# Moving the planned side work of an interleaved attention and Fourier kernel from the start of a section to behind its last tile

## The chip, the cores and the metric

The kernel runs on one core of a Trainium2 chip. The metric is the device time of one execution in microseconds (us); lower is better. Times of unprofiled runs are given as a median over several runs. A profiled execution is a run of its own, with its own time, and its trace gives start and length of every instruction.

A core has five engines, each with its own instruction stream that it works through in order. In the profile PE is TensorE (matmuls), PEld its weight loads, DVE is VectorE, ACT is ScalarE, POOL is GpSimd, and SP is SyncE, which only issues DMAs here. Engines wait for each other through semaphores.

## The reference

Two branches work on the same input `x` (2048 tokens of width 512, float32) and are mixed by a gate per token:

```python
g = _sigmoid((x * gate_w).sum(-1, keepdims=True))
# branch A: Fourier mixing, real part of DFT over tokens of DFT over width
a = einsum("bsd,ed->bse", x, hid_re); b = einsum("bsd,ed->bse", x, hid_im)
A = einsum("ts,bse->bte", seq_re, a) - einsum("ts,bse->bte", seq_im, b)
# branch B: attention with 32 heads of width 16
p = softmax(einsum("bhqd,bhkd->bhqk", q, k) * 16 ** -0.5)
B = einsum("bhqk,bhkd->bhqd", p, v).reshape(B, S, D) @ wo
out = g * A + (1 - g) * B
```

## The kernel before

Every operand that needs more precision than one pass gives is held as a high part and a rest (`hi_lo`: a copy on ACT, a subtraction on DVE or POOL), and a product is three matmuls. The first part of the kernel projects `x` to queries, keys and values and writes queries and keys to DRAM. From there on all stages are interleaved by hand: the schedule is manual, so each engine executes in the order in which the Python code issues.

**Attention.** Two heads make a pair, 16 pairs in all. Pair `p` has its queries and keys in the buffers `qs[p % 2]` and `ks[p % 2]`, 64 rows a head; `load_stacks(p)` (line 196) fills them with 12 DMAs of 128 KB from SP. Three kinds of tiles follow.

- An `a` tile (`a_tile`, line 211) is a product of queries and keys on PE whose row maximum DVE reduces (line 219). When half of a pair's rows are through, `m_parts` and `m_rows` are put into `deferred`; one of them is run at the end of a section. They form the negated maximum and write it as two extra rows into `qs`, by four small DMAs from SP (first head) and four from POOL (second head), line 240.
- An `s` tile (`scores`, line 669) is the product of keys and queries with these rows in it (line 682), and ACT takes the exponential out of PSUM (line 683).
- Value products (`pv`, line 708): for two key blocks ("units"), 8 products of exponentials and values into one PSUM bank (line 718). ACT copies the bank to `oe` (two buffers, line 727), or for the first pair of units of a half straight to `osum` (line 724). The addition of `oe` to `osum` on POOL is put into the list `adds` (line 728) and issued later by `add_sums` (line 738); the last of a half also issues two DMAs that write `osum` to DRAM (line 736).

A unit is one pair, one half of the query rows and one block of 128 keys: 512 units in all. `valued` counts the units whose value products are issued.

**Sections.** `segment` (line 850) runs one pattern of slots: single slots issue a matmul of the other branch (the "d" matmuls of line 378: Fourier products, later output projections) on one half of the PE's rows and, beside it, an `s` or `a` tile of one head on the other half. Each section has 8 `s` and 8 `a` tiles. The last slot, "|", issues what was held back of the Fourier branch (`late`), then `values()` with `pv` for two units. Below, "section N" is the section during which `valued` is N when it starts; it ends with the value products of units N and N+1. 26 sections with the pattern `THIN` (N = 2 to 52) run beside the width transform, 192 with `FULL` (54 to 436) beside the token transform, and 26 with `NINE` (438 to 488) beside projections. Of the eight PSUM banks in use one holds the "d" products; seven rotate over `s` and `a` tiles and value products, in an order that a small planner (`bank`, `read_by`, lines 343 to 359) picks while the code issues; its estimates depend on slots alone.

**Token transform.** Its weights come in chunks: `c_load` (line 319, DMA from SP into `craw`, two buffers) and `c_split` (line 325, high part and rest on POOL, three buffers). After the last matmul of a chunk, `dft_next` (line 426) issues `c_split` for three chunks later and `c_load` for five later, in the even-halved sections (N divisible by 4). Each third such section also ends a row block: ACT takes it out of PSUM (lines 432 and 435), and in the second half of the transform POOL adds the first half's result (line 436).

**Planned steps.** The normalisation of finished attention rows is put into a table `plan`, each entry with the unit at which it is due; `run_plan(u)` issues what is due up to `u + 1`. Before, `run_plan(valued)` stands ahead of every section (line 911).

```python
last = 32 * (4 * ct + n - 1) + 16 * (hf + 1)
at(last + (4 if ct < 3 else 2), sums, hf, ct, n)
at(last + (12 if ct < 3 else 4), inverse, hf, ct, n)
if ct < 3:
    for half in range(2):
        for step, du in enumerate((16, 20, 22)):
            at(last + du + 8 * half, block, step, hf, ct, half)
for p in range(1, NP):
    at(32 * (p - 1), load_stacks, p)
at(456, load_yg, 0, range(3)); at(481, load_yg, 0, range(3, 8))
for step, u in enumerate((486, 490, 494)):
    at(u, last_block, step, 1, 3, nc.gpsimd)
```

`sums` (line 473) gathers the sums of exponentials by two small DMAs into `rc`; `inverse` (line 481) takes the reciprocal on DVE and writes it back by two DMAs; `block` step 0 (line 507) loads a block of rows and its reciprocals by four DMAs into `no`, step 1 multiplies them on POOL (line 515), step 2 casts the product into `nh` on ACT, subtracts on POOL (lines 83 and 84 in `hi_lo`) and stores it by a DMA (line 520). With six combinations of `hf` and `ct` and two halves there are 12 blocks, so 12 casts on ACT, at the starts of sections 134, 142, 150, 158, 262, 270, 278, 286, 390, 398, 406 and 414. `last_block` and `load_yg` do the like for the last pairs and load the mixed Fourier rows.

After the sections comes a tail (line 915 on) for the last units, with its own calls of `add_sums` and `run_plan` ahead of each two units.

Of the kernel before, what the change touches and what calls it, by code (L numbers as in the profile page):

```python
# [31 lines left out]
def mix_kernel(ctx: ExitStack, tc: tile.TileContext, xa_t, xa, wqkv, w_hid, w_seq, wo, gate_w, out):  # L32
# [654 lines left out]
    def pv_last(u):  # L687
        nonlocal now
        blk, k2 = divmod(u - UNITS + 16, 8)
        pt = pts.pop(u)  # L690
        if k2 == 0:
            i, acc = bank()
            free[i] = 1e9
            held[:] = [i]
            last_pairs.append(LastPair(blk, acc))
        acc = last_pairs[-1].acc
        for j in range(4):
            x, h = divmod(j, 2)
            nc.tensor.matmul(acc[32 * j:32 * j + 32], vt[:, 2 * k2 + x, NP - 1, h:h + 32], pt[:, j],  # L699
                             start=k2 == 0, stop=k2 == 7)  # L700
        now += 3.75
        if blk == 0 and k2 == 7:
            last_pairs[0].copy(1)
            free[held[0]] = now + 6
# [3 lines left out]
    def pv(us):  # L708

        nonlocal now  # L710
        i, acc = bank()
        for u in us:
            p, r = divmod(u, 32)
            hf, kt = divmod(r, 16)
            pt = pts.pop(u)
            for j in range(4):
                h = j % 2
                nc.tensor.matmul(acc[32 * j:32 * j + 32], vt[:, kt, p, h:h + 32], pt[:, j],  # L718
                                 start=u == us[0], stop=u == us[-1])
        now += 3.75 * len(us) + 1  # L720
        read_by(i, "s")
        o = osum[:, hf]
        if kt + 1 == len(us):
            nc.scalar.copy(o, acc)
            return
        oe = work.tile([P, 512], F32, name="oe", bufs=2)
        nc.scalar.copy(oe, acc)  # L727
        adds.append(partial(add_sum, o, oe, p, hf, kt == NT - 1))
# [9 lines left out]
    def add_sums():  # L738
        while adds:
            adds.pop(0)()  # L740
# [14 lines left out]
    def issue(x, half, stop=True, late=None):  # L755
        nonlocal now
        now += half is None
        chain, st, mv, after, last = x
        i = chain.mm(st, mv, half, last and stop)
        if stop and after:  # L760
            if last and late is not None:
                late.append(after)
            else:
                after()
        return i

    def pump(gen, n):
        for x in take(gen, n, False):
            issue(x, None)
# [34 lines left out]
    def run_plan(u):  # L804
        for v in sorted(v for v in plan if v <= u + 1):
            for f in plan.pop(v):
                f()
# [19 lines left out]
    users, valued = [], 0  # L827

    def score(kind, h):
        x = next(streams[h][kind == "a"], None)  # L830
        if x:
            if kind == "a":
                i, ps = bank()
                read_by(i, "a")
                users.append((kind, a_tile(*x, ps)))
            else:
                users.append((kind, scores(*x)))

    def values():
        nonlocal valued  # L840
        us = valued, valued + 1
        valued += 2
        add_sums()
        if us[0] < UNITS - 16:
            pv(us)
        else:
            for u in us:
                pv_last(u)

    def segment(pattern, half, ds, stop):  # L850


        nonlocal now
        nonlocal users
        before, users = users, []
        ds, late = iter(ds), []
        for slot in pattern.split():
            if slot == "|":
                for f in late:
                    f()  # L860
                values()
                continue
            now += 1
            if len(slot) == 1:
                x = next(ds, None)
                if x:

                    before = before if x[0].begun else None
                    i = issue(x, half, stop, late)
                    users = []  # L870
                    if before:
                        tc.add_manual_dep(
                            i.ins, dict(before).get("s", before[0][1]).ins.name,
                            mybir.DependencyInfo(mybir.DependencyClass.Sync, mybir.DependencyReason.DATA))
                        before = None
            score(slot[0], 1 - half)
            if len(slot) == 2:
                score(slot[1].lower(), half)
        if deferred:
            deferred.pop(0)()  # L880

    def pairs():

        for i in range(NT - 3):
            yield (THIN,) * 2, take(hid, 12)
        for i in range(2 * NT * 3):
            yield (FULL,) * 2, take(seq, 16)
        for gen, n in ((proj(1, (0, 1, 2), one), 8), (first, 5)):
            for i in range(n):
                yield NINE, take(gen, 9)  # L890
# [5 lines left out]
    for i in range(6):  # L896
        pump(hid, 6)
        if i < 4:
            for kind in "sa":
                for h in range(2):  # L900
                    score(kind, h)
        else:
            if i == 4:
                values()
            for _ in range(2):
                score("s", 0)
                score("a", 0)
    users = []
    for patterns, ds in pairs():
        for half in range(2):  # L910
            run_plan(valued)
            segment(patterns[half], half, ds, half == 1)


# [9 lines left out]
    for u in range(valued + 2, UNITS, 2):  # L924
        add_sums()
        run_plan(u)
        for i in range(4):
            if i == 2:
                pump(*whole[u])
                if u == 506:  # L930
                    last_pairs[0].turn()
                elif u == 508:
                    last_pairs[0].back()
            for h in range(2):
                scores(u + i // 2, i % 2, h)
        if u == 510:
            last_pairs[0].products(())
        values()
# [38 lines left out]
```

## Time and profile before

| | us |
|---|---|
| time, median of 3 unprofiled runs | 1710.47 (1710.4 to 1710.5) |
| the profiled execution's own time | 1713.87 |
| its span, first to last instruction | 1712.1 |
| PE busy (matmuls) | 1693.7 |
| DVE busy | 1376.3 |
| ACT busy | 1247.9 |
| POOL busy | 715.4 |

The span is what the views of the trace divide up; the profiled execution's time has 1.8 us around it. Matmuls overlap, so the share of PE's busy time says that it seldom stands still for long, not that it runs at its peak: a stretch in which matmuls start later shows in the length of a section rather than in idle time. The useful unit of reading is therefore the section, measured from one start of value products (line 718) to the next.

### The profile page before, as it was taken

What the parts mean: (1) busy time and instruction counts of PE and PEld (TensorE: products, weight loads), DVE (VectorE), ACT (ScalarE), POOL (GpSimd) and SP (SyncE); (2) the same over time, 40 slices, a digit from 0 to 9 for tenths busy, and PEclk for the clock granted to TensorE, in tenths of its full rate; (3) what the DMA queues carried; (4) which work ended last, traced back from release to release, by engine and by line L of the source; (5) the groups of instructions that cost most, each with busy time, mean ns of one, the idle gap of its engine ahead of it and who ended that gap; (6) DMA issues with size and microseconds to landing.
All of it is one profiled execution on the core that took longest, in us unless ns stands there. A gap on an engine that the chain in (4) does not pass through costs nothing.

```text
span 1712.1 us, 33831 instructions
## 1 busy us (share of the span) xinstructions
PE 1693.7 (99%) x12731; PEld 1081.6 (63%) x12731; DVE 1376.3 (80%) x2298; ACT 1247.9 (73%) x2472; POOL 715.4 (42%) x775
## 2 busy tenths in 40 slices
PE   8999999999999999999999999999999999999997
PEld 7876666666666666666666666666666656555543
DVE  5448788888888888888888888888888888799943
ACT  5212288887787788778788788778778778778785
POOL 0211144454444455444444555545455555322230
PEclk9999999999999999999999999999999999999999
DMA  8972511314141525232146635241322535560114
GB/s 280 341 173 98 159 16 19 46 32 81 53 80 46 95 89 103 60 67 59 40 92 247 125 94 108 57 87 51 72 73 66 106 100 101 183 151 8 39 27 136
DMA packets 82484, 165.12 MB, mean 96 GB/s; under 512 B 19776, under 2 KB 20032, under 8 KB 78480
## 3 DMA queue, kind: packets, MB, share of 16 engines
q1 hardware_dynamic: 77968, 162.56, 37.1%
q8 instruction: 100, 1.64, 0.4%
q0 software_dynamic: 4352, 0.39, 0.3%
q14 instruction: 64, 0.52, 0.1%
HBM read 107.73 MB, written 54.52 MB: 95 GB/s over the span
## 4 chain that ended last, share of the span: by engine, by line
PE 97%; DVE 1%; DMA 1%; issue 0%; POOL 0%; ACT 0%; SPq 0%; DVEq 0%; POOLq 0%; ACTq 0%
PE d L378 38%; PE t L718 27%; PE t L217 11%; PE t L682 9%; PE t L87 4%; PE t L88 3%; PE t L89 3%; PE t L699 1%; DVE mx L219 1%; PE t L378 0%; DMA qs<-mt 0%; DMA raw<-wqkv 0%; DVE yp L559 0%; PE t L637 0%; DMA o<-osum 0%
## 5 line engine op out<-in xcount | busy, mean ns | idle before, releaser
L219 DVE TENSOR_REDUCE mx<-t 128x1 f32<-128x512 f32 x2048 | 1267.4, 682 | 218.2 <-PE t L217 185.0
L683 ACT ACTIVATE pt<-t 128x512 f32<-128x512 f32 x2048 | 1034.9, 632 | 14.4 <-PE t L682 10.5
L682 PE MATMUL t<-qs,ks 50*128 50x512 f32 x2048 | 745.0, 414 | 3.6 <-DMA qs<-mt 2.4
L217 PE MATMUL t<-ks,qs 48*128 48x512 f32 x2048 | 695.5, 404 | 0.3 <-DVE mx L219 0.2
L378 PE MATMUL d<-xab,ch 64*128 64x512 f32 x2016 | 648.6, 396 | 0.0
L718 PE MATMUL t<-pt,vt 128*32 128x512 f32 x3968 | 478.9, 600 | 0.0
L378 PEld LDWEIGHTS d<-xab,ch 64*128 64x128 f32 x2016 | 367.1, 185 | 131.7 <-issue 90.7
L217 PEld LDWEIGHTS t<-ks,qs 48*128 48x128 f32 x2048 | 366.4, 186 | 79.0 <-DVE mx L219 26.3
L378 PE MATMUL d<-xab,cl 64*128 64x512 f32 x1008 | 399.4, 396 | 0.0
L682 PEld LDWEIGHTS t<-qs,ks 50*128 50x128 f32 x2048 | 367.6, 185 | 39.4 <-ACT pt L683 12.6
L733 POOL TENSOR_TENSOR osum<-osum,oe 128x512 f32<-128x512 f32 x217 | 278.9, 1285 | 124.4 <-ACT oe L727 118.5
L727 ACT COPY oe<-t 128x512 f32<-128x512 f32 x217 | 127.3, 587 | 254.1 <-PE t L718 252.5
L718 PEld LDWEIGHTS t<-pt,vt 128*32 128x32 f32 x3968 | 105.1, 109 | 230.2 <-issue 149.9
L333 POOL CAST ch<-craw 128x512 fp32r<-128x512 f32 x126 | 77.0, 611 | 377.9 <-PE t L682 364.5
L378 PEld LDWEIGHTS d<-xab,cl 64*128 64x128 f32 x1008 | 186.2, 185 | 67.5 <-issue 53.6
L334 POOL TENSOR_TENSOR cl<-craw,ch 128x512 fp32r<-128x512 f32 x126 | 162.1, 1286 | 10.2
L240 POOL DMA_DIRECT2D qs<-mt x128 | 72.0, 568 | 101.5 <-DVE mt L236 94.6
L83 ACT CAST hl<-t 128x512 fp32r<-128x512 f32 x48 | 28.1, 586 | 85.2 <-PE t L89 67.3
L378 PE MATMUL d<-wre,xab 64*128 64x512 f32 (+1 forms) x348 | 85.5, 391 | 0.1
L378 PE MATMUL d<-wo_hl,o_hl 64*128 64x512 f32 (+1 forms) x261 | 69.7, 393 | 0.0
L378 PEld LDWEIGHTS d<-wre,xab 64*128 64x128 f32 (+1 forms) x348 | 64.0, 185 | 7.0 <-issue 1.1
L84 DVE TENSOR_TENSOR hl<-t,hl 128x512 fp32r<-128x512 f32 x48 | 32.9, 687 | 37.6 <-ACT hl L83 37.6
(115 smaller groups left out, 890.8 us busy)
## 6 DMA issues: line engine op xcount, KB each, us to landing
craw<-w_seq SPq DMA_DIRECT2D x128, 256.0 KB
qk<-hl SPq DMA_DIRECT2D x32, 512.0 KB
qs<-qk SPq DMA_DIRECT2D x96, 128.0 KB
ks<-qk SPq DMA_DIRECT2D x96, 128.0 KB
b<-hl SPq DMA_DIRECT2D x16, 512.0 KB
xab<-b SPq DMA_DIRECT2D x16, 512.0 KB
o<-osum SPq DMA_DIRECT2D x62, 128.0 KB
oh<-nh SPq DMA_DIRECT2D x12, 512.0 KB
```

Of the source, the lines that this page charges most:

```text
L87: nc.tensor.matmul(ps, sh, mh, start=first, stop=False)
L217: nc.tensor.matmul(ps, qs[p % 2][r, qt * P:(qt + 1) * P], ks[p % 2][r, kb * 512:(kb + 1) * 512], start=True, stop=True)
L219: user = nc.vector.tensor_reduce(mx[p % 2][:, h, qt, kb:kb + 1], ps, AX.X, ALU.max)
L240: (nc.sync, nc.gpsimd)[h].dma_start(rows.rearrange("v (q b c) -> v b q c", q=8, b=4)[:, b], mt[hf][32 * b + h:32 * b + 32:2])
L333: nc.gpsimd.tensor_copy(h1, raw)
L334: nc.gpsimd.tensor_tensor(l1, raw, h1.bitcast(F32), ALU.subtract)
L378: i = nc.tensor.matmul(self.ps, st[r], mv[r], start=not self.begun, stop=stop)
L682: nc.tensor.matmul(ps, ks[p % 2][rr, kt * P:(kt + 1) * P], qs[p % 2][rr, q0:q0 + 512], start=True, stop=True)
L683: return nc.scalar.activation(pts[u][:, 2 * qb + h], ps, AF.Exp, bias=0.0, scale=DH ** -0.5)
L718: nc.tensor.matmul(acc[32 * j:32 * j + 32], vt[:, kt, p, h:h + 32], pt[:, j], start=u == us[0], stop=u == us[-1])
L727: nc.scalar.copy(oe, acc)
L733: nc.gpsimd.tensor_tensor(o, o, oe, ALU.add)
```

## The change

The call of `run_plan(valued)` ahead of every section goes away. At the "|" slot of `segment`, behind the section's last tile and its held-back Fourier steps, the code now issues the additions of value sums, then the planned steps that are due, then the value products. `valued` has the same value at both places, so an entry that was issued ahead of section N's first tile is now issued behind section N's last tile and ahead of its value products. `add_sums` leaves `values()`; the one other caller of `values()` ahead of the sections gets its own call, and the tail loop has one already. The call of `run_plan` at the start of the tail stays.

```diff
     def values():
         nonlocal valued
         us = valued, valued + 1
         valued += 2
-        add_sums()
         if us[0] < UNITS - 16:
             pv(us)
         else:
@@
             if slot == "|":
                 for f in late:
                     f()
+                add_sums()
+                run_plan(valued)
                 values()
                 continue
@@
             if i == 4:
+                add_sums()
                 values()
@@
         for half in range(2):
-            run_plan(valued)
             segment(patterns[half], half, ds, half == 1)
```

On ACT the order in a section with a cast was: copy of the value sums of the section before, cast, 8 exponentials; it is now: 8 exponentials, cast, copy of this section's value sums. On DVE a planned reciprocal moves from ahead of the section's 8 reductions to behind them (and behind a held-back `finish` where there is one). On POOL planned products and differences now stand behind the section's `c_split` and addition. On SP planned DMAs now stand behind the section's `c_load` and, where a half of a pair is complete, behind the two DMAs that write `osum`. PE executes the same instructions in the same order.

## The prediction

> **What bounds the kernel now.** I read the page's engine totals and the shares of the chain that ended last, then the lengths of single sections.
>
> ```profile
> PE 1693.7 (99%) x12731; PEld 1081.6 (63%) x12731; DVE 1376.3 (80%) x2298; ACT 1247.9 (73%) x2472; POOL 715.4 (42%) x775
> PE 97%; DVE 1%; DMA 1%; issue 0%; POOL 0%; ACT 0%; SPq 0%; DVEq 0%; POOLq 0%; ACTq 0%
> ```
>
> PE holds 97% of the chain, and the change gives PE nothing and takes nothing from it: its instructions and their order stay. So time can only move where PE's matmuls start late because another engine has not freed a bank or delivered an operand. Matmuls overlap, so such a delay shows as a longer section, not as idle PE. I therefore took the windows view, each stretch from one start of value products to the next, for the 12 sections that begin with a cast (one of them and the sum of all 12), and next for the 12 sections just ahead of these (likewise).
>
> ```profile
> 1368.60:1374.93 6.33, 6.33 (x50) 3.30 (x49) 5.48 (x10) 5.03 (x11) 5.59 (x5) 1.00 0.23 81
> ...
> sum 75.86, PE 75.86 PEld 39.35 DVE 65.56 ACT 62.48 POOL 61.68; mean PE 6.32 PEld 3.28 DVE 5.46 ACT 5.21 POOL 5.14
> ```
> ```profile
> 1362.79:1368.60 5.81, 5.81 (x49) 3.81 (x48) 5.50 (x11) 4.49 (x10) 3.59 (x6) 1.00 0.03 3
> ...
> sum 69.84, PE 69.84 PEld 45.17 DVE 61.54 ACT 53.90 POOL 35.56; mean PE 5.82 PEld 3.76 DVE 5.13 ACT 4.49 POOL 2.96
> ```
>
> The first number after a stretch is its length. Sections with a cast take 6.32 us in the mean, their neighbours 5.82: 0.50 us each, 75.86 - 69.84 = 6.02 us in all. PE counts as busy throughout in both. Why it is the cast: ACT's and DVE's timelines in section 398, which lies between the value products that start at 1368.60 and 1374.93.
>
> ```profile
> 1370.65 0.59 ACT L727 COPY oe<-t 128x512 f32<-128x512 f32 x1 [1.30 <-PE t L718]
> 1371.13 0.62 ACT L83 CAST nh<-no 128x512 fp32r<-128x512 f32 x1
> 1371.65 4.02 ACT L683 ACTIVATE pt<-t 128x512 f32<-128x512 f32 x8
> 1376.97 0.59 ACT L727 COPY oe<-t 128x512 f32<-128x512 f32 x1 [1.30 <-PE t L718]
> ```
> ```profile
> 1371.24 4.99 DVE L219 TENSOR_REDUCE mx<-t 128x1 f32<-128x512 f32 x8 [0.82 <-PE t L217]
> 1377.56 0.69 DVE L219 TENSOR_REDUCE mx<-t 128x1 f32<-128x512 f32 x1 [1.33 <-PE t L217]
> ```
>
> A section is a ring on ACT: copy of the value sums, 8 exponentials, 1.30 us of waiting for the value products, next copy. The cast sits between the copy and the exponentials and starts them 0.52 us late (1371.65 against 1371.13). The exponentials free the banks, so PE's tiles and the value products behind them slip by as much, and DVE waits 1.33 instead of 0.82 us for the next section's first tile.
>
> **The change part by part.** *The 12 casts* go behind the 8 exponentials and ahead of the next copy, where ACT waits 1.30 us: 1371.65 + 4.02 = 1375.67 to 1376.97. A cast of 0.62 us fits, if its operand is there. What it removes is 0.50 us a cast, 6.02 us. What it costs in the new place lies between nothing and the 0.50 us that it costs now (then nothing is gained). I take nothing, because the gap is twice the cast.
>
> The operand is the product of line 515 on POOL, which moves too: from ahead of the tiles two units earlier to behind that section's `c_split` and addition. It is latest where that section also ends a row block in the second half of the transform (sections 268, 388 and 412, each with its cast one section later). Section 388 ends with the value products that start at 1344.81; POOL's timeline from there, the group with the product's length, and section 390's window:
>
> ```profile
> 1346.19 1.28 POOL L436 TENSOR_TENSOR y<-y,yr 128x512 f32<-128x512 f32 x1 [2.34 <-ACT y L435]
> ...
> 1350.59 1.29 POOL L84 TENSOR_TENSOR nh<-no,nh 128x512 fp32r<-128x512 f32 x1
> ```
> ```profile
> L515 POOL TENSOR_TENSOR no<-no 128x512 f32<-128x512 f32 x12 | 15.5, 1293 | 0.1
> ```
> ```profile
> 1344.81:1351.13 6.32, 6.32 (x49) 3.24 (x49) 5.46 (x10) 5.58 (x12) 4.86 (x5) 1.00 0.37 100
> ```
>
> After the change the product takes the slot at 1350.59 and ends at 1351.88. Without the delay section 390 lasts 5.82 us, so its value products start at 1350.63; the copy follows such a start by 1376.97 - 1374.93 = 2.04 us, at 1352.67. The cast can run from 1351.88 to 1352.50: it fits with 0.17 us to spare. In the nine other cases no row-block addition (1.28 us) stands ahead of the product, which is then some 1.3 us earlier at least. Should POOL be late in the three, a cast costs at most its 0.50 us: 1.5 us for the bound. The moved differences (1.29 us each) and additions lie on POOL, 42% busy; the ring shown waits for no moved one of them while `oe` has its second buffer.
>
> In a sentence that the sum does not need: the Trainium skill, "TensorE: Matmul & The Clock Gate" (the architectural detail of the array), says that ScalarE's queue is strictly first in, first out; the rows agree (the exponentials stood behind the cast), and by that rule a late product now holds back the copy as well, which is the second rival's mechanism.
>
> *The reciprocals.* Six (line 484) stand in `FULL` sections; section 396 in the second table has one in its 5.50 us of DVE and lasts 5.81, so it hides in DVE's 0.82 us wait for a new section's first tile. Behind the section before or behind its own, the wait is the same: nothing. The two of section 484 are paid:
>
> ```profile
> 1619.07 4.87 DVE L219 TENSOR_REDUCE mx<-t 128x1 f32<-128x512 f32 x8 [0.43 <-PE t L682]
> 1623.86 1.11 DVE L488 RECIPROCAL rc<-rc 48x64 f32<-48x64 f32 x2
> 1625.01 4.87 DVE L219 TENSOR_REDUCE mx<-t 128x1 f32<-128x512 f32 x8
> 1629.91 0.75 DVE L559 SCALAR_TENSOR_TENSOR yp_qs<-d,omg,yp_qs 128x512 f32<-128x512 f32 x1
> 1630.96 1.29 DVE L219 TENSOR_REDUCE mx<-t 128x1 f32<-128x512 f32 x2 [0.30 <-PE t L682]
> ```
> ```profile
> 1610.72:1616.67 5.95, 5.95 (x43) 3.44 (x42) 5.47 (x10) 4.64 (x11) 1.29 (x1) 1.00 0.83 246
> 1622.03:1628.58 6.55, 6.29 (x44) 3.36 (x43) 6.49 (x12) 4.93 (x11) 3.06 (x3) 1.00 0.06 15
> ```
>
> They lengthen section 484 from 5.95 to 6.55 us: 0.60, and that goes. In the new place they follow the `finish` at 1629.91, where DVE has only 0.30 us of waiting left: 1.11 - 0.30 = 0.81 us paid in section 486. Net +0.2 us; the ends are -0.6 (absorbed) and 1.11 - 0.60 = +0.5.
>
> *The loads.* A stack load is 12 DMAs on SP, now behind `c_load` and the two `osum` writes. SP in section 416 before:
>
> ```profile
> 1424.47 0.55 SPq L204 DMA_DIRECT2D qs<-qk  x1
> ...
> 1432.01 0.30 SPq L205 DMA_DIRECT2D ks<-qk  x1
> 1433.07 0.35 SPq L323 DMA_DIRECT2D craw<-w_seq  x1
> 1434.20 1.43 SPq L736 DMA_DIRECT2D o<-osum  x2
> ```
>
> Issue takes 1432.31 - 1424.47 = 7.84 us. It will start after this section (5.82 us later), after POOL's work at its end (at worst 1350.59 - 1344.81 = 5.8 us, as above) and the writes (1.43): some 13 us later. Pair 14's first `a` tile comes three sections and four tiles after the end of section 416: each head has 20 `a` tiles of its old pair left when section 416 starts, and takes 8 in every second section. Counted from that end, the first head needs its rows at about 3 x 5.82 + 2 + 2 = 21 us; its half of the load is issued by 5.8 + 1.4 + 3.9 = 11 us, or 14 with a block's four DMAs ahead. Some 5 us are left for landing even then, also for the second head, which needs its half a section later. Nothing, with the lateness of a rival as the other end. `c_load` slips at most those 7.84 us and serves a `c_split` two chunks on (a chunk is 12 of the 16 matmul slots of two sections, so 2 x 8.7 us): nothing. The `sums`, write-backs, block loads and stores shift as a train that keeps its spacings, and `load_yg` leads its readers by a section or more: nothing. `add_sums` keeps its place ahead of the value products.
>
> One train runs into steps that do not move: the last block, due at 490 at the start of the tail. Its product on POOL stands ahead of the four DMAs that carry the last rows of `qs`; SP, POOL, and the exponentials that follow the first product with those rows:
>
> ```profile
> 1624.42 1.21 SPq L489 DMA_DIRECT2D r<-rc  x2
> ...
> 1634.08 0.59 SPq L503 DMA_DIRECT2D o_raw<-r  x1
> ```
> ```profile
> 1641.23 2.39 POOL L537 TENSOR_TENSOR o_raw<-o_raw 128x1024 f32<-128x1024 f32 x1
> 1643.53 2.26 POOL L240 DMA_DIRECT2D qs<-mt  x4
> ```
> ```profile
> 1654.15 2.08 ACT L683 ACTIVATE pt<-t 128x512 f32<-128x512 f32 x4
> ```
>
> The reciprocals move from 1623.86 to 1629.91 + 0.75 - 0.60 = 1630.06, so the last load ends its issue 6.2 us later, at 1640.9, and lands after the 1641.23 at which POOL now multiplies. That is a new wait of some 2 us (estimate), and the row DMAs end at 1643.53 + 2.26 + 2 = 1647.8. Their reader stands at 1654: some 6 us for landing, so nothing; if that cover went, POOL's lateness would be paid in full, 2 us.
>
> **Sum:** -6.02 + 0.2 = -5.8 us, on the profiled span 1712.1 to 1706.3. The unprofiled median 1710.47 lies 1.6 us below that span; the same subtraction gives 1704.7.
>
> **The rivals.** *The product is late*: POOL finishes the three close ones after the copy's turn, and casts cost there what they cost now. For it: 0.17 us of slack. Against: nine others have over a microsecond. Price up to 1.5 us: 1706.2. Were all products late by half, 12 x 0.25 = 3.0 us: 1707.7. *The cast pays wherever it stands*, as ACT's load would limit the section: no gain, 1710.7 with the +0.2. Against: 1.30 us of waiting in each ring. *A transfer now comes too late (slower).* This happens once already, where two extra rows of `qs` land late:
>
> ```profile
> 1463.24:1473.75 10.51, 8.08 (x50) 4.94 (x49) 6.50 (x12) 5.08 (x10) 4.96 (x5) 0.78 0.61 202
> 1473.75:1480.67 6.92, 6.92 (x49) 3.96 (x49) 3.71 (x7) 4.36 (x9) 1.30 (x1) 0.84 0.13 19
> ```
> ```profile
> PE t L682 <- DMA qs<-mt: 2.4, 1, 2.4
> ```
>
> The two sections cost 10.51 + 6.92 - 2 x 5.82 = 5.8 us: 2.4 us of waiting and a granted clock of 0.78 and 0.84. If stack loads slip 5 us more than worked out, in two of their 14 places, it is +11.6 - 5.8: 1716.3. Against: no stack load is waited for now. (The Trainium skill, same page, Part 1 on the clock gate, puts the throttle behind about 3.4 us of idleness; here 2.4 us sufficed. By the rule a shorter wait would cost itself alone.) *That stop disappears*, if shifted DMAs no longer meet the rows: a further -5.8, 1698.9; nothing planned stands near it.
>
> **How the numbers follow.** Forecast 0.84 (1704.7), product late 0.06, casts still paid 0.03, transfers late 0.04, stop gone 0.03. Its own bounds run from -6.02 - 0.6 = -6.6 (1703.8) to -6.02 + 1.5 + 0.5 = -4.0 (1706.5); reaching halfway to the other cases I say 1703.6 to 1707.3. About 0.2%, 3.4 us, is what a measurement can tell from no change: faster is everything under 1707.05, the forecast, the vanished stop and most of the late products: 0.91; same 0.05, slower 0.04.
>
> **What would show it.** In the twelve sections: ACT's row order exponentials, cast, copy, a length of 5.82, DVE's first wait 0.82 again. Section 484 at 5.95 and 486 about 0.8 longer. No PE wait on `ks<-qk`. It is wrong if the twelve stay near 6.3, if ACT waits on POOL ahead of a cast, or if a new section of over 6 us stands at a pair's first `a` tile.

## The result, and the profile after

| | before | after |
|---|---|---|
| time, median (us) | 1710.47 (1708.73 to 1713.71, 15 runs) | 1706.86 (1705.68 to 1708.68, 15 runs) |
| the profiled execution: time, span (us) | 1713.87, 1712.1 | 1707.86, 1706.1 |
| ratio of the times | | 0.9979, 95% interval [0.9971, 0.9987] |

The gain is 3.6 us by the medians; the interval makes it 2.2 to 5.0. Timed again beside other kernels the same change gave 1706.76 against 1711.26, ratio 0.9974 [0.9964, 0.9985], 4.5 us. The forecast was 5.8.

The page of the changed kernel, engine totals and shares of the chain that ended last:

```profile
PE 1688.0 (99%) x12731; PEld 1085.1 (64%) x12731; DVE 1378.9 (81%) x2298; ACT 1248.7 (73%) x2472; POOL 715.8 (42%) x775
PE 96%; DMA 2%; DVE 1%; issue 0%; SPq 0%; POOL 0%; ACT 0%; DVEq 0%; POOLq 0%; ACTq 0%
```

PE's busy time falls by 5.7 us with the same 12731 matmuls, so they follow each other sooner; but the chain now has 2% of DMA where it had 1%. The twelve cast sections in the windows view (after the stretch: its length, busy time of PE, PEld, DVE, ACT and POOL, granted clock, share of the DMA engines, GB/s), section 398 and the sum of all twelve:

```profile
1364.35:1370.18 5.83, 5.83 (x50) 3.65 (x49) 5.43 (x11) 4.54 (x10) 4.40 (x4) 1.00 0.20 53
...
sum 69.90, PE 69.90 PEld 45.01 DVE 61.02 ACT 56.49 POOL 54.40; mean PE 5.83 PEld 3.75 DVE 5.08 ACT 4.71 POOL 4.53
```

75.86 - 69.90 = 5.96 us are gone. ACT's timeline at the end of section 398 shows why, and DVE's shows the wait for the next section's first tile:

```profile
1366.88 4.03 ACT L683 ACTIVATE pt<-t 128x512 f32<-128x512 f32 x8
1370.78 0.64 ACT L83 CAST nh<-no 128x512 fp32r<-128x512 f32 x1
1372.17 0.59 ACT L727 COPY oe<-t 128x512 f32<-128x512 f32 x1 [0.75 <-PE t L718]
```
```profile
1372.82 1.42 DVE L219 TENSOR_REDUCE mx<-t 128x1 f32<-128x512 f32 x2 [0.83 <-PE t L217]
```

The cast stands behind the exponentials, and of the 1.30 us in which ACT waited for the value products 0.75 us are left: the cast took the rest. DVE waits 0.83 us again.

Then where is the difference between 5.8 and the measured 3.6 to 4.5? I compared all 247 stretches from one start of value products to the next in the two traces (244 sections and three stretches of the tail). Outside the twelve, only six changed by more than 0.1 us. The windows of these six (sections 230, 266, 366, 430, 484 and 486) after the change, with 432, which belongs to 430:

```profile
874.32:880.41 6.09, 6.09 (x50) 3.72 (x49) 5.21 (x10) 4.50 (x10) 2.49 (x2) 1.00 1.01 115
979.44:985.78 6.34, 6.27 (x49) 3.72 (x48) 5.10 (x11) 4.73 (x10) 2.91 (x4) 1.00 0.96 284
1270.99:1277.10 6.11, 6.11 (x50) 3.69 (x49) 5.26 (x10) 5.08 (x11) 5.19 (x6) 1.00 0.33 107
1457.57:1467.68 10.11, 8.07 (x50) 4.92 (x49) 6.50 (x12) 5.08 (x10) 4.97 (x5) 0.78 0.65 209
1467.68:1474.67 6.99, 6.99 (x49) 3.94 (x48) 3.69 (x7) 4.34 (x9) 1.30 (x1) 0.82 0.13 19
1616.05:1622.01 5.96, 5.96 (x44) 3.44 (x43) 5.48 (x10) 4.63 (x11) 1.30 (x1) 1.00 0.02 6
1622.01:1628.01 6.00, 5.74 (x41) 3.24 (x41) 5.94 (x11) 4.51 (x10) 3.06 (x3) 1.00 0.02 4
```

Section 266 before the change, for comparison (the windows of 430, 432 and 484 before stand in the prediction):

```profile
982.43:988.25 5.82, 5.82 (x50) 3.79 (x49) 5.09 (x11) 4.52 (x10) 2.91 (x4) 1.00 0.19 48
```

| section | before | after | difference |
|---|---|---|---|
| the twelve with a cast | 75.86 | 69.90 | -5.96 |
| 230 and 366 | 5.81 + 5.82 | 6.09 + 6.11 | +0.57 |
| 266 | 5.82 | 6.34 | +0.52 |
| 430 and 432 | 10.51 + 6.92 | 10.11 + 6.99 | -0.33 |
| 484 and 486 | 6.55 + 5.35 | 5.96 + 6.00 | +0.06 |

The table adds to -5.1 us, and all 247 stretches to -4.75, since the others drift by up to 0.1 us each, +0.4 in all. Of the span's 6.0 us another 1.2 lie ahead of the first value products (214.30 before, 213.13 after), in a part that the change doesn't touch; over the fourteen profiles this moment lies between 212.8 and 214.3. Without 430 and 432, which are treated below, the table adds to -4.8 us.

**Section 266.** It begins with the first `a` tile of pair 9's second head (the first head's stands in section 264). The chain of waits of the changed kernel there, and the first and last issue of that pair's stack load on SP:

```profile
968.74 9.22 DMA qs<-qk
977.97 4.13 DMA rc<-o
982.10 0.46 PE t L217
```
```profile
965.79 0.53 SPq L204 DMA_DIRECT2D qs<-qk  x1
...
973.15 0.72 SPq L205 DMA_DIRECT2D ks<-qk  x1
```

An `a` tile (line 217) stands behind transfers. The landings, read from the completion records of the trace (the chain's names for them are inferred), for the 12 DMAs of this load:

```
          issue, first to last     landed: first DMA, sixth, last    last: issue to landing
before    950.64 to 958.76         955.35   960.59   967.07          8.31
after     965.79 to 973.87         970.08   976.77   981.96          8.09
```

The load's DMAs land about 1.1 us apart, and the last one lands 8 us after its issue. It landed at 981.96, the tile started at 982.09; the value products ahead of it had started at 979.44 and the "d" matmul of its slot at 981.64, so it was wanted at about 981.6.

**Sections 484 and 486.** DVE after the change:

```profile
1623.23 0.74 DVE L559 SCALAR_TENSOR_TENSOR yp_qs<-d,omg,yp_qs 128x512 f32<-128x512 f32 x1
1623.89 1.12 DVE L488 RECIPROCAL rc<-rc 48x64 f32<-48x64 f32 x2
1625.04 4.88 DVE L219 TENSOR_REDUCE mx<-t 128x1 f32<-128x512 f32 x8
```

The reciprocals stand behind the `finish` and DVE has no wait left behind them, as forecast.

### The profile page after: what moved, and what is told of

It is laid out like the page before. It is cut to its first block, busy times and chain, and to the rows that moved or that the text cites. A ratio compares the mean times of both kernels' runs of the same rounds, so it can differ in the third digit from the quotient of the medians.

```text
span 1706.1 us, 33838 instructions
## 1 busy us (share of the span) xinstructions
PE 1688.0 (99%) x12731; PEld 1085.1 (64%) x12731; DVE 1378.9 (81%) x2298; ACT 1248.7 (73%) x2472; POOL 715.8 (42%) x775
## 4 chain that ended last, share of the span: by engine, by line
PE 96%; DMA 2%; DVE 1%; issue 0%; SPq 0%; POOL 0%; ACT 0%; DVEq 0%; POOLq 0%; ACTq 0%
PE d L378 39%; PE t L718 26%; PE t L217 11%; PE t L682 9%; PE t L87 4%; PE t L88 3%; PE t L89 3%; PE t L699 1%; DVE mx L219 1%; DMA qs<-qk 1%; DMA rc<-o 0%; PE t L378 0%; DMA qs<-mt 0%; DMA raw<-wqkv 0%; DVE yp L559 0%
```

## The experiments

All ratios are to the kernel before on the same chip, by medians, with a 95% interval.

| kernel | time (us) | ratio |
|---|---|---|
| e1: only the casts moved | 1705.57 | 0.9967 [0.9955, 0.9979] |
| e2: change, stack loads ahead | 1705.24 | 0.9965 [0.9953, 0.9977] |
| e3: only the stack loads moved | 1711.56 | 1.0003 [0.9994, 1.0011] |
| e4: change, four row DMAs from SP | 1700.75 | 0.9939 [0.9927, 0.9952] |
| e5: e2 with e4's edit | 1702.81 | 0.9951 [0.9938, 0.9963] |
| e6: before, cast on POOL | 1705.78 | 0.9965 [0.9951, 0.9979] |
| e7: change, product a section later | 1709.23 | 0.9984 [0.9975, 0.9993] |
| e8: change, stack loads two sections later | 1761.47 | 1.0287 [1.0264, 1.0310] |
| e9: e1 with e4's edit | 1702.38 | 0.9947 [0.9933, 0.9961] |
| e10: e9, and pair 14's rows too | 1701.23 | 0.9939 [0.9925, 0.9953] |
| e11: the change again | 1706.76 | 0.9974 [0.9964, 0.9985] |
| e12: e2 again | 1706.33 | 0.9969 [0.9958, 0.9981] |

**The parts of the change, e1 to e3.** The planned steps are split into two tables; `ahead` runs one of them ahead of the section as before the change, `run_plan` the other behind the last tile.

```diff
     def at(u, f, *args):
-        plan.setdefault(u, []).append(partial(f, *args))
+        behind = f is block and args[0] == 2       # e1: casts only
+        behind = f is not load_stacks              # e2: all but the stack loads
+        behind = f is load_stacks                  # e3: the stack loads only
+        (plan if behind else first_plan).setdefault(u, []).append(partial(f, *args))
@@
         for half in range(2):
+            ahead(valued)
             segment(patterns[half], half, ds, half == 1)
```

> Only step 2 of the blocks (cast on ACT, difference on POOL, store) is issued behind a section's last tile; every other planned step stays ahead of the first tile, as before the change. Theory (the gain is the place of the cast in ACT's ring, the stack loads give a little of it back): the 12 cast sections go from 6.32 to 5.82 us, section 266 stays at 5.82, sections 484 and 486 stay at 6.54 and 5.35; all sections together 6.0 us shorter than before, ratio 0.9965. Rival (the gain comes from moving the whole train of loads, products and casts together): well under 6 us, ratio 0.998 or more.

> The changed kernel, but the stack loads of query and key rows stay ahead of the section's first tile. Theory: section 266 goes back from 6.34 to 5.82 us, the loads land 6 to 13 us earlier, nothing else changes: 0.5 us less than the changed kernel in the sections, ratio to the kernel before 0.9965 to 0.9975. Rival (section 266 is chance and has nothing to do with the loads): 266 stays above 6.2 or another section takes its place.

> Only the stack loads are issued behind the section's last tile; all other planned steps stay ahead. Theory: the 12 cast sections stay at 6.32, the load of pair 9 lands within a microsecond of its first reader, and section 266 is at 6.0 to 6.5 or just not; sections together 0 to 0.6 us longer than before, ratio 1.000. Rival (late loads are what the median lost against my forecast): 2 us or more slower, ratio above 1.001, with waits at several pairs' first a tiles.

The twelve sections (sum) in e1 and in e3:

```profile
sum 69.91, PE 69.91 PEld 45.56 DVE 59.72 ACT 56.59 POOL 49.19; mean PE 5.83 PEld 3.80 DVE 4.98 ACT 4.72 POOL 4.10
```
```profile
sum 75.79, PE 75.79 PEld 39.47 DVE 65.62 ACT 62.48 POOL 62.01; mean PE 6.32 PEld 3.29 DVE 5.47 ACT 5.21 POOL 5.17
```

In e1 and in e2 all twelve sections last 5.8 us; e1 leaves 230, 266, 366, 484 and 486 as before, and its time is 5.6 us below the kernel before. In e2 section 266 is back at 5.82, 230 and 366 stay 0.28 longer, 484 and 486 are as in the change, and its time is 5.9 us below the kernel before. In e3 the twelve stay at 6.32, section 266 at 5.83 (the load landed 1.03 us ahead of the value products' start there), and the time doesn't move. So the casts alone carry the gain; the stack loads bring nothing and can cost. That e2 loses 0.6 us to e1 in sections 230 and 366 doesn't show in the medians, whose intervals are wider than that.

**Is it ACT's ring? e6.** The kernel before, with nothing moved; POOL makes the cast.

```diff
-            hi_lo(hl[:, 0], hl[:, 1], t[:, 0], nc.gpsimd)
+            nc.gpsimd.tensor_copy(hl[:, 0], t[:, 0])
+            nc.gpsimd.tensor_tensor(hl[:, 1], t[:, 0], hl[:, 0].bitcast(F32), ALU.subtract)
```

> The kernel before, with the 12 casts as copies on POOL instead of ACT, at their old place ahead of a section's tiles; nothing is moved. Theory (the 6 us were ACT's ring: the cast between the copy and the exponentials): the twelve sections last 5.82 us as in the change, the sum is some 6 us shorter than before, ratio about 0.9965, and POOL gets 12 more instructions of about 1.3 us each that nothing in the ring waits for. Sections 484 and 486 stay as before (6.55 and 5.35). Rival (the gain came from the order on POOL or SP, or from sections that would have been shorter anyway behind the last tile): the twelve stay at 6.32, ratio 1.000.

The windows of the twelve sections (sum) and the group of the casts in e6's profile:

```profile
sum 69.92, PE 69.92 PEld 44.78 DVE 59.62 ACT 56.53 POOL 62.96; mean PE 5.83 PEld 3.73 DVE 4.97 ACT 4.71 POOL 5.25
```
```profile
L519 POOL CAST nh<-no 128x512 fp32r<-128x512 f32 x12 | 7.3, 607 | 0.0
```

The same 69.9 us as the change gives, without moving a step, though POOL is busy for 5.25 of each 5.83 us. A POOL cast takes 0.61 us, half of what the expectation said. So the 6 us were the cast's place in ACT's ring: they go when the cast leaves it, with every other step where it was.

**Where the cast's operand is late, e7.**

```diff
-        for step, du in enumerate((16, 20, 22)):
+        for step, du in enumerate((16, 22, 22)):
```

> The changed kernel with the product of a block (line 515) issued right ahead of its cast, a section later than in the change. Theory (strict order on ACT makes a late operand of the cast hold back the copy of the value sums; POOL is late only where a row block has just ended): sections 270, 390 and 414 get about 1.3 us longer than 5.82, the place of one more addition on POOL, with ACT waiting on POOL ahead of the cast; the other nine stay at 5.82. Time about 3.8 us above the changed kernel, ratio to before about 1.000. Rival (the wait is absorbed by the ring's 1.3 us of waiting for the value products, or all twelve are late): no section changes and the ratio stays at 0.997 to 0.998, or all twelve grow by some 0.5 to 1.3 us and the ratio is 1.002 to 1.007.

ACT, then POOL in e7 at the value products that end section 390 (start 1346.93); for comparison POOL and ACT there in the changed kernel (start 1346.90); and e7's windows of section 392 and the sum of 272, 392 and 416:

```profile
1349.59 0.62 ACT L83 CAST nh<-no 128x512 fp32r<-128x512 f32 x1 [1.92 <-POOL no L515]
1350.12 0.58 ACT L727 COPY oe<-t 128x512 f32<-128x512 f32 x1
```
```profile
1348.28 1.28 POOL L515 TENSOR_TENSOR no<-no 128x512 f32<-128x512 f32 x1
```
```profile
1346.89 1.28 POOL L515 TENSOR_TENSOR no<-no 128x512 f32<-128x512 f32 x1
```
```profile
1348.20 0.62 ACT L83 CAST nh<-no 128x512 fp32r<-128x512 f32 x1 [0.55 <-POOL no L515]
1348.89 0.59 ACT L727 COPY oe<-t 128x512 f32<-128x512 f32 x1
```
```profile
1346.93:1353.85 6.92, 6.83 (x49) 3.25 (x48) 5.63 (x11) 5.00 (x11) 5.26 (x6) 1.00 0.77 220
...
sum 20.74, PE 20.57 PEld 9.71 DVE 16.87 ACT 15.03 POOL 15.77; mean PE 6.86 PEld 3.24 DVE 5.62 ACT 5.01 POOL 5.26
```

The product starts 1.39 us later, ACT waits for it with the copy queued behind the cast, and the section that follows grows from 5.83 to 6.92: three times 1.08 us, and nowhere else. The theory holds, with the cost a section later than I had written, because the copy that is held back belongs to the start of the next ring. 1.39 us of lateness cost 1.08, so some 0.3 us of it cost nothing. The median rises by 2.5 us over e11, not by 3.2 and not by the 3.8 expected; in e7's profile sections 230, 266 and 366 were at 5.82 to 5.86, and section 436 rose by 0.27.

**How near the stack loads are to too late, e8.**

```diff
-    at(32 * (p - 1), load_stacks, p)
+    at(32 * (p - 1) + (4 if p > 1 else 0), load_stacks, p)
```

> The changed kernel with the stack loads of pairs 2 to 15 due four units (two sections) later. The first a tile of a pair had its rows 0.7 to 10 us before it needed them in the changed kernel. Theory (a stack load that starts ever later turns into a wait of PE on qs or ks, which is what cost 0.5 us in section 266 of the changed kernel): the loads land 8 to 12 us later, the rows are late at most pairs by 0 to 10 us, waits on qs<-qk or ks<-qk appear in the chain, and the sum is 20 to 60 us longer, with a lowered clock behind the longer waits. Ratio 1.01 to 1.035. Rival (SP would still run ahead, or a tiles have more room than the landing times say): no wait on these rows at more than two pairs, ratio below 1.002.

e8's longest waits of PE on these loads, and its windows of sections 392 and 394:

```profile
PE t L217 <- DMA ks<-qk: 30.1, 14, 5.1
```
```profile
1392.59:1405.40 12.81, 7.73 (x50) 4.61 (x49) 6.52 (x12) 5.58 (x11) 6.05 (x7) 0.85 0.98 140
1405.40:1412.66 7.26, 7.26 (x50) 3.81 (x49) 3.83 (x8) 4.38 (x9) 2.46 (x4) 0.80 0.88 225
```

14 waits on `ks<-qk`, 30.1 us in all, and 55.8 us more over all sections than in the change: the granted clock is 0.85 and 0.80 in the two sections shown. Two sections were more than all the room there was. Pair 9's load, whose moment of landing varies from run to run, gives the point at which it begins to cost (us from the start of the value products ahead of section 266):

```
                      e3      e7      e4      e11     change   e8
last DMA landed     -1.03    1.43    1.65    2.18     2.52     3.95
section 266 lasts    5.83    5.82    5.81    5.98     6.34     9.52
```

Before the change it landed 15.4 us ahead of that start. In e8 the first head's half is late as well (section 264 lasts 8.61 us), so its column is more than one wait.

**The stop at section 430, e4, e9, e10 and e5.** The forecast counted 430 and 432 as constant. POOL and SP in the changed kernel:

```profile
1453.95 1.71 POOL L240 DMA_DIRECT2D qs<-mt  x3 [0.53 <-DVE mt L236]
1458.30 0.56 POOL L240 DMA_DIRECT2D qs<-mt  x1 [2.64 <-issue]
```
```profile
1456.63 2.54 SPq L462 DMA_DIRECT2D wo_hl<-wo  x4
```

The first three row DMAs of the second head landed 1.1 us after their issue; the fourth, issued while SP was issuing four weight loads of 512 KB, took 4.6 us. It landed at 1463.44, and PE's tile started right behind:

```profile
1463.57 0.76 PE L682 MATMUL t<-qs,ks 50*128 50x512 f32 x1 [2.04 <-DMA qs<-mt]
```

POOL issues this fourth DMA 2.64 us after the third; what it waits for there isn't shown. In e4 SP issues these rows itself, ahead of the weight loads.

```diff
-                (nc.sync, nc.gpsimd)[h].dma_start(rows...
+                (nc.sync, nc.sync if (p, hf) == (13, 1) else nc.gpsimd)[h].dma_start(rows...
```

> The changed kernel, with one more edit: the four small DMAs that write the extra rows of the second head of pair 13, second half, are issued by SP and no longer by POOL, so they stand ahead of the four 512 KB loads of the output weights on SP. Theory (the long stop at section 430 is the fourth of these row DMAs being caught behind the weight loads): sections 430 and 432 go from 10.1 and 7.0 to about 5.8 each, the granted clock stays at 1.0 there, 5.4 us less than the changed kernel, ratio to the kernel before 0.9945 to 0.995. Rival (the stop is instruction fetch or another wait at that place): unchanged.

e4's SP timeline and its windows of 430 and 432:

```profile
1452.39 5.56 SPq L240 DMA_DIRECT2D qs<-mt  x8
1458.04 2.54 SPq L462 DMA_DIRECT2D wo_hl<-wo  x4
```
```profile
1456.25:1462.06 5.81, 5.81 (x49) 3.80 (x49) 4.96 (x10) 4.51 (x10) 3.39 (x3) 1.00 0.43 138
1462.06:1467.87 5.81, 5.81 (x49) 3.81 (x49) 4.98 (x10) 4.51 (x10) 1.30 (x1) 1.00 0.85 250
```

The stop is gone, and the ratio, 0.9939, is a little below the 0.9945 to 0.995 that were expected. The scatter shrinks with it: e4's five times lie within 1.2 us (1699.92 to 1701.14) and e10's five within 1.3, where the fifteen of the kernel before spread over 5.0 us (1708.73 to 1713.71). Over ten profiles with the weight loads in the way 430 and 432 together took 13.9 (e1) to 18.2 us (e3), which makes a difference of medians uncertain by more than 1 us here. Whether the size of the stop depends on the change these profiles don't settle: one profile a kernel is one draw, and the two longest are of the kernels with ACT's casts ahead (before, 17.4, and e3, 18.2). By the ratios, taking the stop away is worth 0.0035 to 0.0040 to the change (the first timing and e11 against e4) and 0.0028 to e1 (against e10).

> Only the casts (with their differences and stores) are moved behind the last tile, and the extra rows of the second head in pair 13's second half are written from SP instead of POOL. Theory (the parts add up: casts -5.9 us; no cost at 266, 230, 366, 484 and 486; the stop at sections 430 and 432 is gone whatever its size by chance is): twelve sections at 5.82, sections 430 and 432 at 5.8 each, no PE wait on qs<-mt; time about 1699.5 us, ratio 0.993 to 0.994, at or slightly below the changed kernel with rows from SP (1700.75). Rival (the saved time of 430 depends on where the loads stand): a stop of 2 us or more stays at 430, ratio 0.996 to 0.998.

> Only the casts moved, and the extra rows of the second head from SP in two halves of pairs (pair 13's second and pair 14's first half), so that neither is behind other DMAs. Theory (section 446 lost 1.0 us in the kernel with the one half from SP because the fourth row DMA was issued on POOL while stack loads were already in flight): 446 back to 5.36, sections 430 and 432 at 5.81, time 1.0 us below that kernel, ratio 0.9935 to 0.9942. Rival (SP's queue, now held by the row DMA's wait, makes the stack loads or the rows late): 446 stays above 5.9 or another section grows, ratio 0.995 or more.

> The changed kernel with the stack loads ahead and with pair 13's second-half rows from SP. It differs from the changed kernel with rows from SP only in where the stack loads stand. Theory (stack loads ahead of a section are in flight when the fourth row DMA of section 444 is issued): section 266 at 5.82, 446 at 6.4 instead of 5.36, time 0.5 to 1.2 us above the kernel with rows from SP, ratio 0.994 to 0.995. Rival (446 has another cause, such as the place of the reciprocals): 446 at 5.36 and the ratio at 0.9935 or below.

e9 is 1.6 us slower than e4, and not faster: section 446 takes 6.39 instead of 5.36 us. Its windows in e4 and in e9, then POOL and PE of e9 there:

```profile
1502.08:1507.44 5.36, 5.36 (x42) 3.24 (x41) 4.94 (x9) 4.38 (x10) 3.15 (x3) 1.00 0.01 0
```
```profile
1502.99:1509.38 6.39, 5.43 (x41) 2.99 (x41) 5.97 (x11) 4.27 (x10) 3.15 (x3) 1.00 0.96 131
```

```profile
1503.70 0.56 POOL L240 DMA_DIRECT2D qs<-mt  x1 [2.64 <-ACT pt L683]
```
```profile
1508.75 0.47 PE L682 MATMUL t<-qs,ks 50*128 50x512 f32 x1 [0.96 <-DMA qs<-mt]
```

Again a fourth row DMA, issued at 1503.70 while a stack load that began at 1502.71 is in flight, and a tile that waits for it. By the completion records it landed 4.35 us after its issue; the same DMA of e4, issued by POOL at the same place with no load in flight, landed after 1.13. In e10 the rows of this half come from SP as well (`(p, hf) in ((13, 1), (14, 0))`), ahead of the load; in e5 the change keeps the stack loads ahead, with e4's one half from SP. Windows of section 446 in e10 and in e5:

```profile
1502.68:1508.12 5.44, 5.44 (x42) 3.41 (x41) 5.01 (x9) 4.47 (x10) 1.29 (x1) 1.00 0.64 98
```
```profile
1503.03:1509.86 6.83, 5.45 (x42) 2.99 (x41) 6.25 (x11) 4.27 (x10) 3.15 (x3) 1.00 0.99 135
```

5.44 against 6.83: e10's 1701.23 is 1.15 us below e9 (1.0 expected), and e5's 1702.81 is 2.1 above e4 (0.5 to 1.2 expected), of which section 446 makes 1.47. So once the stop at 430 was gone, moving the stack loads behind did help in this one place: they no longer met the rows of section 444. e4 and e10 are the fastest kernels of the study, with one ratio of 0.9939. e10 is the one I would keep, since its stack loads have their old slack.

**The loads' share of the median, e11 and e12.**

> The changed kernel itself, timed beside the three others of this call. Theory (it gives back part of the casts' gain at section 266, where the stack load lands late, and 0.28 us each at 230 and 366): 0.6 to 1.6 us slower than the kernel with the stack loads ahead, ratio to before 0.9965 to 0.9980. Rival (the 2.2 us missing from the forecast are the varying stop at section 430 alone): the two agree within 0.3 us.

> The changed kernel with the stack loads ahead of the section, as before, beside the changed kernel on one chip. Theory (the loads' move costs where a load lands late): section 266 at 5.82, 230 and 366 at 6.1, ratio about 0.9965, 0.6 to 1.6 us below the changed kernel. Rival: no difference to it beyond 0.3 us.

e12 is 0.43 us below e11, between the 0.6 to 1.6 of the theory and the 0.3 of the rival: the medians don't settle it. The sections do, as far as they go: 266 at 5.98 in e11 (6.34 in the first profile) and at 5.85 in e12. In the five profiles with the stack loads behind the last tile (the change, e11, e3, e4 and e7; e8 aside) pair 9's load cost 0.5, 0.2 and three times nothing.

## Why the prediction came out as it did

The measured 1706.86 us lies in the stated range of 1703.6 to 1707.3, but not within the bounds that the sum itself had (1703.8 to 1706.5): it is inside because the range was stretched halfway to the rivals, and that much is luck. In the sections, which the working is about, 4.8 us are gone, and that is within the sum's 4.0 to 6.6.

Two of the three things named as signs of being wrong did appear. ACT waited for a late operand ahead of the cast in the three close places (0.55 to 0.57 us, at the ends of sections 270, 390 and 414), at no cost. The prediction's own times have this wait: the exponentials end 1.30 us ahead of the copy, at 1351.37, and the product at 1351.88, so the sign was drawn too wide. And a new section of over 6 us, 266, stands at a pair's first `a` tile; that was a miss, answered below under the loads.

**The casts** (-6.02): right in place, sign and size (-5.96), and e6 and e7 show the mechanism, ACT's ring, from both sides.

**The late product** (0.17 us to spare in three sections): right. ACT waited 0.55 us for POOL, and the copy started 0.69 us after the cast, where in e7, held back by the cast alone, it starts after 0.53: 0.16 us were to spare. e7 shows that the mechanism of the first rival, the late product, is real and begins within 0.3 us: its price, had it come true, is 1.08 us a place at 1.39 us of lateness, not the 0.5 us at which I bounded it, because the copy behind the cast is held back too.

**The reciprocals** (+0.2): -0.59 in section 484 (0.60 foretold) and +0.65 in 486 (0.81 foretold), +0.06. The train into the tail came as foretold: POOL waits for the last block's rows,

```profile
1636.64 2.39 POOL L537 TENSOR_TENSOR o_raw<-o_raw 128x1024 f32<-128x1024 f32 x1 [1.29 <-DMA o_raw<-r]
```

1.29 us (2 estimated), and the tail's stretches stay as they were.

**The loads**: this is the step that failed. "Some 5 us are left for landing even then, also for the second head, which needs its half a section later. Nothing". The issue times were about right (at pair 9 the load started 9.6 us after its section's end, where I had 5.8 + 1.4 = 7.2, or some 10 with a block's DMAs ahead). But I set those 5 us against nothing: the landing had no price. The load's last DMA lands 8 us after its issue, and it did so before the change, too, hidden by 15 us of slack. With 7.8 us left at pair 9, from the last issue at 973.87 to 981.64, there was nothing to spare: +0.52 in the profile, +0.16 in another, nothing in three. One reading was wrong as well: only the first head has 20 `a` tiles of its old pair left, the second has 16, so it needs its rows some 4 us after the first and not a whole section; that is the head that waited. The rival of late transfers was priced as a stop with a lowered clock; as it came, a wait of half a microsecond cost itself alone.

**Not in the sum at all**: sections 230 and 366, +0.57 us, from ACT's instruction stream (last section). I had looked at what ACT executes and when, and not at the change's other effect on ACT: 12 semaphore waits fewer (3056 instructions instead of 3068), so that all that follows has other numbers.

**The stop at 430**: a chance of 0.03 was given to its vanishing. It didn't vanish, but I had taken it as a constant from one profile, and it is the largest difference between profiles of these kernels. With -5.96 + 0.06 + 0.52 + 0.57 = -4.8 us from the sections, the measured 3.6 (2.2 to 5.0) and 4.5 (2.6 to 6.2) fit; the rest between them isn't resolved by these medians. A stop at 430 that is longer in the changed kernel than before would account for it; no run shows that, and none rules it out.

## What to carry to other kernels

In an engine's ring, put an extra instruction where the engine waits longest, and make sure that its operand is ready earlier than that, since all that is queued behind it waits too. When DMAs are moved, price the landing of the last one of the batch, from completion records, and not its issue. A small DMA that a tile waits for is better issued ahead of large ones (1.1 against 4.4 to 4.6 us to landing here), and a stop that a single profile shows may be one draw out of a wide spread.

## What the runs showed of the hardware that was not expected

**A number in ACT's stream.** The copies of value sums start 0.04 us after the semaphore wait ahead of them (median of the 210 to 234 copies a kernel that stand behind a wait). A few start 0.32 us after. ACT in the changed kernel, section 230:

```profile
876.65 0.59 ACT L727 COPY oe<-t 128x512 f32<-128x512 f32 x1 [1.59 <-PE t L718]
```

1.59 us instead of 1.30. Counting ACT's instructions from the start of the trace:

```
            instruction   remainder by 128   start after the wait (us)
change         1471             63                0.32
change         2239             63                0.33
e7             2623             63                0.32
e6             2751             63                0.32
```

In these three kernels, and in e2, e4, e5, e8, e11 and e12, every copy that is late by this has the remainder 63. Before the change, and in e1, e3, e9 and e10, no copy of value sums behind a short wait falls on one, and none is late. e7 has 12 instructions fewer on ACT than the change, and in it sections 230 and 366 are back at 5.82 and 5.86 while section 436, at instruction 2623, is 0.27 longer. So the delay goes with the number and moves with it; why isn't shown.

**Landing.** The 12 DMAs of 128 KB of a stack load land 1.1 us apart; a row DMA that takes 1.1 us alone took 4.6 us beside four loads of 512 KB and 4.35 us beside a stack load.

**The clock.** PE's stop at 430 (length of the section less PE's busy time) and the granted clock, in e1 and in e2:

```profile
1456.66:1464.75 8.09, 6.22 (x49) 3.69 (x48) 5.33 (x10) 4.97 (x10) 4.96 (x5) 1.00 0.79 262
```
```profile
1457.21:1465.48 8.27, 6.22 (x49) 3.68 (x49) 5.33 (x10) 4.97 (x10) 4.96 (x5) 1.00 0.76 256
```

Stops of 1.87 and 2.05 us left the clock at 1.00; the changed kernel's stop of 10.11 - 8.07 = 2.04 us brought 0.78, and 0.82 in the next section. The length of the stop alone doesn't decide. Part of the scatter is here: in e1 and e2, without a lowered clock, 430 and 432 took 13.9 and 14.1 us, and in the eight profiles with one 16.2 to 18.2. (The Trainium skill, "TensorE: Matmul & The Clock Gate", Part 1 on the clock gate, puts the throttle behind about 3.4 us of idleness; the lowered clock behind 2.04 us here does not agree with it.)
